# Half of a first stage's tiles transposed by DMA instead of TensorE, with q's relu on ScalarE and row statistics one tile per step

## The chip, the cores and the metric

The kernel runs on one core of one Trainium2 chip. The metric is the device time of one launch in microseconds (us). Before the change it was 854.06 us, the median of three runs (852.98 to 855.43). The span in a profile is some 2 us shorter than the time of the same execution.

## The reference, cut to what matters

One transformer block, forward and backward: linear attention of 32 heads and a gated MLP, each behind a layer norm without weights. Inputs are bf16; S is 2048, D is 640, F is 1728. The kernel returns the output and six gradients; the change touches only the beginning of the forward pass.

```python
def _A_ref(x, wqkv, wo):                      # x is already layer-normed
    qkv = (x @ wqkv) ...                      # split in q, k, v and heads
    phi = lambda t: jnp.where(t > 0, t + 1, jnp.exp(t)) + 1e-6
    pq, pk = phi(q), phi(k)
    kv = jnp.einsum("bhsd,bhse->bhde", pk, v)
    z = jnp.einsum("bhsd->bhd", pk)
    num = jnp.einsum("bhqd,bhde->bhqe", pq, kv)
    den = jnp.einsum("bhqd,bhd->bhq", pq, z)[..., None] + 1e-6
    o = num / den
    ...
h = x + _A_ref(_layernorm(x), A_wqkv, A_wo)
h2 = h + _B_ref(_layernorm(h), B_w1, B_w3, B_w2)   # silu(gate) * up, then w2
...
_out, _vjp = jax.vjp(_f, A_x, A_wqkv, A_wo, B_w1, B_w3, B_w2)
```

## The kernel before

Rows are handled in 16 tiles of 128. In the first stage each tile is normalised (`xn`, VectorE), transposed (`pqT`, TensorE and a ScalarE copy), and multiplied with wqkv. phi(k) and v stay in groups of four tiles for the kv products. phi(q) goes to DRAM (`pq_d`) and comes back transposed, in chunks of four tiles, by one DMA transposition each. `dma` and `dmaT` both issue from SyncE, so all these transfers stand in one queue in program order.

```python
    def p1_norm(t):
        xns[t] = p1.tile([P, D], BF16, name="xn", bufs=2)
        ln1.norm(xns[t][:], x_sb[:, t, :], t)

    def p1_tr(t):
        xn = xns.pop(t)
        tr = ps.tile([P, DT, P], BF16, name="tr", bufs=2)
        for c in range(DT):                               # DT = 5
            T.transpose(tr[:, c, :], xn[:, c * P:(c + 1) * P], ident[:])
        A.copy(out=pqT[:, :, t * P:(t + 1) * P], in_=tr[:])

    def phi(acc, dst):
        mq = p1.tile([P, D], BF16, name="mq", bufs=3)
        A.activation(two(mq[:]), acc[:, :, 0:HD], AF.Exp)
        V.tensor_scalar(out=mq[:], in0=mq[:], scalar1=1.0, scalar2=1e-6, op0=ALU.min, op1=ALU.add)
        V.scalar_tensor_tensor(out=two(dst), in0=acc[:, :, 0:HD], scalar=0.0, in1=two(mq[:]), op0=ALU.max,
                               op1=ALU.add)

    def q_store(t, pq):
        dma(out=pq_v[:, t, :], in_=pq)
        if t % TPC == TPC - 1:                            # TPC = 4
            load_pqT(t // TPC)                            # DMA transposition of 640 KB
    # ... cut: kv_group, zero_pads, the list of trickled weight loads ...
    for t in range(ST):                                   # ST = 16
        g, i = divmod(t, TPC)
        # ... cut ...
        k = p1_mm(t, D)
        if t + 2 < ST:
            p1_norm(t + 2)
        phi(k, pkc[g][:, i, :])
        if t + 1 < ST:
            p1_tr(t + 1)
        if i == 0 and g > 0:
            kv_group(g - 1, False)
        v = p1_mm(t, 2 * D)
        A.copy(out=va[g % 2]..., in_=v...)
        if 4 <= t < 12:
            q_tile(t - 4)
        if t % 2 == 0 and t + 4 < ST:
            ln1.run(x_sb, t + 4, t + 6)
        # ... cut ...
        if i == TPC - 1:
            dma(out=pk_v[:, sl, :], in_=pkc[g][:])
            dma(out=va_v[:, sl, :], in_=va[g % 2][:])
        elif t >= 2 and trickle:
            trickle.pop(0)()                              # the next weight load
```

After the MLP, the first weight gradient needs `hb`, a DMA transposition of 2 MB; the remaining products of the output run meanwhile on TensorE.

```python
    def load_hh(b):
        f0, fw = blk[b]
        hb[b] = U2.tile([P, ST, 512], BF16, name="hb", tag="ABCA"[b])
        dmaT(out=hb[b][:, :, 0:fw], in_=hh_d[f0:f0 + fw, :])

    load_hh(0)
    for _ in o2_steps(SC - 1, A.dma_start, "nd"):
        drain(1)
```

Of the kernel before, what the change touches and what calls it, by code (L numbers as in the profile page):

```python
# [9 lines left out]
P = 128  # L10
BF16 = mybir.dt.bfloat16
F32 = mybir.dt.float32
ALU = mybir.AluOpType
AF = mybir.ActivationFunctionType
# [4 lines left out]
S, D, H, F = 2048, 640, 32, 1728  # L19
# [3 lines left out]
ST, DT, CT = S // P, D // P, CP // P  # L23
FT, FP = 14, 1792
FL = F - 13 * P
W, SC, TPC = 512, 4, 4
HD = D // 2
# [36 lines left out]
def kernel(  # L64
# [19 lines left out]
    V, A, T, G, SY = nc.vector, nc.scalar, nc.tensor, nc.gpsimd, nc.sync  # L84
    dma, dmaT = SY.dma_start, SY.dma_start_transpose
# [22 lines left out]
    def pool(name, side="left", space=None):  # L108
        kw = dict(space=space) if space is not None else dict(side=side)
        return tc.alloc_tile_pool(name=name, bufs=1, reuse_waits="tile", **kw)  # L110
# [4 lines left out]
    x_sb = U1.tile([P, ST, D], BF16, name="x_sb", tag="S0")  # L115
# [32 lines left out]
    ln1, ln2 = Stats("ln1"), Stats("ln2")  # L148
# [3 lines left out]
    p1 = pool("p1", "right")  # L152
# [20 lines left out]
    def make_mask(m):  # L173
        a, b = M_H[m]
        v = mask[:, m, 0:M_W[m]]
        G.memset(v, 1.0)
        v = v.rearrange("p (h e) -> p h e", e=DA)

        G.affine_select(out=v, in_=v, pattern=[[-DH, b - a], [0, DA]], compare_op=ALU.is_ge, fill=0.0,
                        base=m * P - a * DH, channel_multiplier=1)  # L180
        G.affine_select(out=v, in_=v, pattern=[[DH, b - a], [0, DA]], compare_op=ALU.is_gt, fill=0.0,
                        base=a * DH + DH - m * P, channel_multiplier=-1)
# [6 lines left out]
    pqT = U1.tile([P, DT, S], BF16, name="pqT", tag="Q")  # L189
# [6 lines left out]
    def load_pqT(c):  # L196
        dmaT(out=pqT[:, :, c * W:(c + 1) * W], in_=pq_d[c * W:(c + 1) * W, :])
# [11 lines left out]
    pkc = {}  # L209
    xns = {}  # L210

    def p1_norm(t):
        xns[t] = p1.tile([P, D], BF16, name="xn", bufs=2)
        ln1.norm(xns[t][:], x_sb[:, t, :], t)

    def p1_tr(t):
        xn = xns.pop(t)
        tr = ps.tile([P, DT, P], BF16, name="tr", bufs=2)
        for c in range(DT):
            T.transpose(tr[:, c, :], xn[:, c * P:(c + 1) * P], ident[:])  # L220

        A.copy(out=pqT[:, :, t * P:(t + 1) * P], in_=tr[:])  # L222

    def p1_half(acc, t, n0):
        for c in range(DT):
            T.matmul(acc, lhsT=pqT[:, c, t * P:(t + 1) * P], rhs=wqkv[:, c, n0:n0 + HD], start=(c == 0),  # L226
                     stop=(c == DT - 1))

    def p1_mm(t, n0):
        acc = ps.tile([P, 2, 512], F32, name="big", bufs=3)  # L230
        for j in range(2):
            p1_half(acc[:, j, 0:HD], t, n0 + j * HD)
        return acc

    def two(ap):
        return ap.rearrange("p (j n) -> p j n", j=2)

    def phi(acc, dst):
        mq = p1.tile([P, D], BF16, name="mq", bufs=3)
        A.activation(two(mq[:]), acc[:, :, 0:HD], AF.Exp)  # L240
        V.tensor_scalar(out=mq[:], in0=mq[:], scalar1=1.0, scalar2=1e-6, op0=ALU.min, op1=ALU.add)
        V.scalar_tensor_tensor(out=two(dst), in0=acc[:, :, 0:HD], scalar=0.0, in1=two(mq[:]), op0=ALU.max,
                               op1=ALU.add)

    def q_store(t, pq):
        dma(out=pq_v[:, t, :], in_=pq)
        if t % TPC == TPC - 1:
            load_pqT(t // TPC)

    def q_tile(t):  # L250
        pq = p1.tile([P, D], BF16, name="pq", bufs=3)
        phi(p1_mm(t, 0), pq[:])
        q_store(t, pq[:])

    def kv_group(g, last):
        kv = ps.tile([P, 2, 512], F32, name="big", bufs=3)
        for i in range(TPC):
            for m, (a, b) in enumerate(M_H):
                bank, off = KV_SLOT[m]
                T.matmul(kv[:, bank, off:off + M_W[m]], lhsT=pkc[g][:, i, m * P:(m + 1) * P],  # L260
                         rhs=va[g % 2][:, i, a * DA:b * DA], start=(i == 0 and off == 0), stop=(i == TPC - 1),
                         skip_group_check=True)
        for bank, w in ((0, sum(M_W[0:3])), (1, sum(M_W[3:5]))):
            if g == 0:
                V.tensor_copy(out=kvacc[:, bank, 0:w], in_=kv[:, bank, 0:w])
            else:
                V.tensor_tensor(out=kvacc[:, bank, 0:w], in0=kvacc[:, bank, 0:w], in1=kv[:, bank, 0:w],
                                op=ALU.add)
        if last:
            for m, (a, b) in enumerate(M_H):  # L270
                bank, off = KV_SLOT[m]
                V.tensor_tensor(out=kvbd[:, m, a * DA:b * DA], in0=kvacc[:, bank, off:off + M_W[m]],
                                in1=mask[:, m, 0:M_W[m]], op=ALU.mult)
# [22 lines left out]
    for t in range(ST):  # L296
        g, i = divmod(t, TPC)
        if i == 0:
            pkc[g] = p1.tile([P, TPC, D], BF16, name="pkc", bufs=2)
        k = p1_mm(t, D)  # L300
        if t + 2 < ST:
            p1_norm(t + 2)
        phi(k, pkc[g][:, i, :])
        if t + 1 < ST:
            p1_tr(t + 1)
        if i == 0 and g > 0:
            kv_group(g - 1, False)
        v = p1_mm(t, 2 * D)
        A.copy(out=va[g % 2][:, i, 0:C].rearrange("p (j h e) -> p j h e", j=2, e=DA)[:, :, :, 0:DH],
               in_=v[:, :, 0:HD].rearrange("p j (h e) -> p j h e", e=DH))  # L310
        if 4 <= t < 12:
            q_tile(t - 4)
        if t % 2 == 0 and t + 4 < ST:
            ln1.run(x_sb, t + 4, t + 6)
        if 2 <= t < 2 + DT:
            make_mask(t - 2)
            G.memset(kvbd[:, t - 2, :], 0.0)
        if i == TPC - 1:
            sl = slice(g * TPC, (g + 1) * TPC)
# [3 lines that stand above are left out]
            trickle.pop(0)()  # L323
# [150 lines left out]
    def drain(n):  # L474
        for _ in range(min(n, len(later))):
            later.pop(0)()
# [74 lines left out]
    for c in range(SC):  # L551
        hhT[c] = pa.tile([P, FT, W], BF16, name="hhT", bufs=2)
        o2 = o2_steps(c - 1) if c > 0 else None

        def run_side(pos, fc):
            if c + 1 < SC:
                for f, i in sorted(sides[c][pos].get(fc, ()), key=lambda x: x[1]):
                    f((c + 1) * TPC + i)

        for fc in range(FT):  # L560
            mlp(c, fc, lambda: run_side(0, fc))
            drain(1)
            if o2 and not (c == SC - 1 and fc == 5):
                next(o2, None)
            run_side(1, fc)
            drain(1)
            if c == 0 and fc in (1, 4, 7):
                a, b = {1: (0, 4), 4: (4, 8), 7: (8, 13)}[fc]
                dma(out=w2[:, a:b, :], in_=B_w2[a * P:b * P, :].rearrange("(c p) n -> p c n", p=P))
                if fc == 7:  # L570
                    dma(out=w2[0:FL, FT - 1, :], in_=B_w2[(FT - 1) * P:F, :])
            if fc == (9 if c == 0 else 3) and c + 1 < SC:
                load_g2T(c + 1)
            if c == SC - 1 and fc == 0:
                g2 = U1.tile([P, ST, D], BF16, name="g2", tag="Q")
                tail = U2.tile([P, DT, P], BF16, name="w13tail", tag="g2T", bufs=2)
            if c == SC - 1 and fc in (1, 2, 5, 6):
                i = (1, 2, 5, 6).index(fc)
                dma(out=g2[:, i * TPC:(i + 1) * TPC, :], in_=goS[:, i * TPC:(i + 1) * TPC, :])
            if c == SC - 1 and fc == 8:  # L580
                dma(out=tail[:, :, 0:FL], in_=B_w1[:, F - FL:F].rearrange("(c p) f -> p c f", p=P))
                dma(out=tail[:, :, FL:P], in_=B_w3[:, 0:P - FL].rearrange("(c p) f -> p c f", p=P))
            if c == SC - 1 and fc == 9:
                woT = U1.tile([P, DT, D], BF16, name="woT", tag="W6")
                dmaT(out=woT[:], in_=A_wo[:, :])
# [71 lines left out]
    for fc in range(FT - 1):  # L657
# [3 lines left out]
        acc = ps.tile([P, 2, 512], F32, name="gw", bufs=4)  # L661
# [249 lines left out]
    a, b, c = ST - 1, ST - 2, ST - 3  # L911
# [34 lines left out]
    for m, (e0, e1) in enumerate(M_H):  # L946
        bank, off = KV_SLOT[m]
        V.tensor_tensor(out=gkv_b[:, m, e0 * DA:e1 * DA], in0=gkv[:, bank, off:off + M_W[m]],
                        in1=mask[:, m, 0:M_W[m]], op=ALU.mult)
# [65 lines left out]
    for t in range(ST):  # L1015
        c, i = divmod(t, TPC)
        acc = [d_acc(), d_acc()]
# [123 lines left out]
```

## Time and profile before

| What | Value | Where it is read |
|---|---|---|
| time | 854.06 us | median of three runs |
| span, TensorE busy | 851.9 us, 838.2 us | the page |
| TensorE idle at the start | 5.7 us | its list of waits |
| 20 to 72 us: TensorE, VectorE, ScalarE | 51.99, 38.04, 30.13 of 52 us | the table by stage |
| DMA share in the same stretch | 0.88 | the table by stage |

The lines themselves stand in the prediction below. They are read so: first who is busy all the time (TensorE), then in which stretch the change acts and what else is full there (the DMA), then what a transpose displaces on TensorE (0.28 us per tile). `nd` is the product that gives the reference's num and den.

### The profile page before, as it was taken

The numbers are of one execution on the slowest core, as the hardware profiler recorded it, in microseconds if no ns is written. First come the engines' busy times: TensorE is split into PE (matmuls) and PEld (weight loads), VectorE is DVE, ScalarE is ACT, GpSimd is POOL, SyncE is SP. The second block draws the span as 40 slices with busy tenths as digits, with TensorE's granted clock in tenths as the row PEclk, the third lists the DMA queues.
The fourth block names the chain that finished last, engine by engine and source line by source line (L and its number), as shares of the span: only waits on it lengthen the run. The fifth ranks groups of instructions, "written<-read, shape, count | busy, mean of one in ns | idle before, by whom it ended". The sixth has DMA issues, their size and how long they took to land.

```text
span 851.9 us, 14886 instructions
## 1 busy us (share of the span) xinstructions
PE 838.2 (98%) x5920; PEld 545.6 (64%) x5948; DVE 416.4 (49%) x945; ACT 322.2 (38%) x608; POOL 29.1 (3%) x51
## 2 busy tenths in 40 slices
PE   6999999999999999999999999999999999999998
PEld 4777654555555555777777777777877777655554
DVE  7786699778678566300146656654413343300000
ACT  4557866655555665011111111122522333311111
POOL 1410000000000000000000000000000000000000
PEclk9999999999999999999999999999999999999999
DMA  9979579364364465999789999979666897677671
GB/s 281 266 241 277 155 209 245 104 182 144 89 174 147 140 199 153 238 236 250 194 162 193 192 209 206 179 141 261 152 128 131 191 207 160 153 161 163 149 180 36
DMA packets 339573, 155.04 MB, mean 182 GB/s; under 512 B 242224, under 2 KB 338224, under 8 KB 339504
## 3 DMA queue, kind: packets, MB, share of 16 engines
q1 hardware_dynamic: 310688, 141.13, 68.4%
q10 hardware_dynamic: 28816, 12.97, 8.2%
q8 instruction: 46, 0.75, 0.4%
q14 instruction: 23, 0.19, 0.1%
HBM read 45.20 MB, written 50.02 MB: 112 GB/s over the span
## 4 chain that ended last, share of the span: by engine, by line
PE 85%; DMA 3%; DVE 2%; ACT 1%; issue 0%; SPq 0%; DVEq 0%; ACTq 0%
PE job L972 21%; PE mm L417 18%; PE ghn L720 11%; PE gxn L1062 8%; PE o L508 7%; PE gw L664 7%; PE gwo L827 3%; PE h L777 2%; PE at L374 2%; DMA ghT<-g_h 1%; DMA ggb<-gg_d 1%; PE mm L226 1%; PE dkv L1021 1%; DMA g2T<-in_grad_out_dram 1%; PE dkv L808 1%; PE h L808 1%
## 5 line engine op out<-in xcount | busy, mean ns | idle before, releaser
L972 PE MATMUL job<-gb,hnN 128*128 128x432 bf16 x640 | 117.0, 346 | 0.0
L720 PEld LDWEIGHTS <-ggb 128*128 128x128 bf16 x864 | 83.0, 98 | 31.6 <-DMA ggb<-gg_d 0.7
L972 PEld LDWEIGHTS <-hnN 128*128 128x128 bf16 x640 | 62.6, 98 | 54.1
L417 PE MATMUL mm<-pqT,w 128*128 128x512 bf16 x396 | 95.7, 379 | 0.5
L417 PEld LDWEIGHTS <-w 128*128 128x128 bf16 x540 | 52.4, 98 | 60.7 <-issue 0.2
L976 ACT CAST obs<-job 128x432 bf16<-128x432 f32 (+1 forms) x70 | 33.3, 475 | 123.8 <-PE job L972 123.8
L417 PE MATMUL mm<-g2T,w2T 128*128 128x512 bf16 x265 | 68.5, 379 | 1.4 <-DMA g2T<-in_grad_out_dram 0.7
L508 PE MATMUL o<-w,hhT 128*128 128x320 bf16 x448 | 67.5, 299 | 0.0
L1062 PE MATMUL gxn<-wqT,gT 128*128 128x320 bf16 x480 | 67.3, 299 | 0.0
L720 PE MATMUL ghn<-w13a,ggb 128*128 128x320 bf16 x448 | 65.6, 299 | 0.0
L720 PE MATMUL ghn<-w13b,ggb 128*128 128x320 bf16 x416 | 63.5, 299 | 0.4 <-DMA ggb<-gg_d 0.4
L226 PE MATMUL big<-wqkv,pqT 128*128 128x320 bf16 x400 | 58.6, 303 | 1.5 <-ACT pqT L222 0.8
L508 PEld LDWEIGHTS <-hhT 128*128 128x128 bf16 x448 | 43.8, 98 | 23.6
L226 PEld LDWEIGHTS <-pqT 128*128 128x128 bf16 x480 | 46.4, 99 | 19.5 <-issue 1.3
L1062 PEld LDWEIGHTS <-gT 128*128 128x128 bf16 x480 | 47.0, 98 | 18.2
L972 PEld LDWEIGHTS <-g 128*128 128x128 bf16 x480 | 46.6, 98 | 17.5
L664 PE MATMUL gw<-g,hb 128*128 128x320 bf16 x416 | 57.7, 299 | 0.0
L434 ACT CAST ghh<-mm 128x512 bf16<-128x512 f32 x56 | 32.8, 586 | 63.7 <-PE mm L417 62.3
L743 ACT ACTIVATE y<-wb,s,ln_rs 128x640 bf16<-128x640 f32 x32 | 29.5, 920 | 66.8 <-DVE wb L739 66.8
L664 PEld LDWEIGHTS <-hb 128*128 128x128 bf16 x416 | 40.3, 98 | 15.3
L731 ACT ACTIVATE gs<-ghn 128x640 bf16<-128x640 f32 x16 | 11.3, 704 | 88.4 <-PE ghn L720 75.3
L448 ACT ACTIVATE sig<-mm 128x512 bf16<-128x512 f32 x56 | 33.5, 598 | 28.9 <-PE mm L417 27.0
(138 smaller groups left out, 1067.1 us busy)
## 6 DMA issues: line engine op xcount, KB each, us to landing
hh_d<-hhT SPq DMA_DIRECT2D x24, 256.0 KB, 2.4
gg_d<-gate SPq DMA_DIRECT2D x24, 256.0 KB, 2.5
gg_d<-up SPq DMA_DIRECT2D x24, 256.0 KB, 2.2
ggb<-gg_d SPq DMA_DIRECT2D x6, 896.0 KB, 9.1
ggb<-gg_d SPq DMA_DIRECT2D x6, 832.0 KB, 7.8
out_dram<-obs ACTq DMA_DIRECT2D x40, 108.0 KB, 2.7
ggb<-gg_d SPq DMA_DIRECT2D x2, 1728.0 KB, 13.4
va_d<-va SPq DMA_DIRECT2D x4, 768.0 KB, 6.0
```

The lines of the kernel that those rows point to most:

```text
L226: T.matmul(acc, lhsT=pqT[:, c, t * P:(t + 1) * P], rhs=wqkv[:, c, n0:n0 + HD], start=(c == 0), stop=(c == DT - 1))
L417: T.matmul(acc[:], lhsT=w[:, c, fc * P:(fc + 1) * P], rhs=rhs[:, c, :], start=(c == 0), stop=(c == DT - 1))
L434: A.copy(out=ghh[n // 2][:, n % 2, :], in_=acc[:])
L448: A.activation(sig[:, i, :], gp[:], AF.Sigmoid)
L508: T.matmul(o2["ps"][:, 0:HD], lhsT=hhT[c][:, fc, i * P:(i + 1) * P], rhs=w2[:, fc, j * HD:(j + 1) * HD], start=(fc == 0), stop=(fc == FT - 1))
L664: T.matmul(acc[:, j, 0:HD], lhsT=hb[b][:, t, i * P:(i + 1) * P], rhs=g2[:, t, j * HD:(j + 1) * HD], start=(t == 0), stop=(t == ST - 1))
L720: T.matmul(acc[:, j, 0:HD], lhsT=ggb[t // 2][:, k, lo:lo + P], rhs=rhs[:, j * HD:(j + 1) * HD], start=(k == 0), stop=(k == NG - 1))
L743: A.activation(out=y[:], in_=wb[:], func=AF.Identity, bias=s[:, 3:4], scale=st.rs[:, t:t + 1])
L827: T.matmul(acc[m][:, j, 0:HD], lhsT=o_sb[:, t, m * P:(m + 1) * P], rhs=g_h[:, t, j * HD:(j + 1) * HD], start=(t == 0), stop=(t == ST - 1))
L972: T.matmul(acc[:, 0:n], lhsT=lhs[:, t, m * P:(m + 1) * P], rhs=rhs(t), start=(t == 0), stop=(t == ST - 1))
L976: A.copy(out=ob, in_=acc[:, 0:n])
L1062: T.matmul(acc[:, j, 0:HD], lhsT=gT[t][:, k, :], rhs=wqT[:, k, j * HD:(j + 1) * HD], start=(k == 0), stop=(k == 14))
```

## The change

The intent is to take 40 transposes off TensorE, which is busy 98% of the span, by letting DMA transpose the normalised tiles 8 to 15 straight into `pqT`. q's relu moves to ScalarE to unload VectorE. The statistics are spread one tile per step, and the loads of transposed q are moved out of the way of the new transfers. This is the whole diff, but for context lines.

```diff
+    XT_DMA = 8
+
     def p1_norm(t):
-        xns[t] = p1.tile([P, D], BF16, name="xn", bufs=2)
+        xns[t] = p1.tile([P, D], BF16, name="xn", bufs=4)
         ln1.norm(xns[t][:], x_sb[:, t, :], t)
+        if t >= XT_DMA:
+            dmaT(out=pqT[:, :, t * P:(t + 1) * P], in_=xns.pop(t)[:])
...
-    def phi(acc, dst):
+    def phi(acc, dst, relu=False):
         mq = p1.tile([P, D], BF16, name="mq", bufs=3)
         A.activation(two(mq[:]), acc[:, :, 0:HD], AF.Exp)
+        if relu:
+            rq = p1.tile([P, D], BF16, name="rq", bufs=3)
+            A.activation(two(rq[:]), acc[:, :, 0:HD], AF.Relu)
         V.tensor_scalar(out=mq[:], in0=mq[:], scalar1=1.0, scalar2=1e-6, op0=ALU.min, op1=ALU.add)
+        if relu:
+            V.tensor_tensor(out=dst, in0=mq[:], in1=rq[:], op=ALU.add)
+            return
...
     def q_store(t, pq):
         dma(out=pq_v[:, t, :], in_=pq)
-        if t % TPC == TPC - 1:
-            load_pqT(t // TPC)

     def q_tile(t):
         pq = p1.tile([P, D], BF16, name="pq", bufs=3)
-        phi(p1_mm(t, 0), pq[:])
+        phi(p1_mm(t, 0), pq[:], True)
...
-        if t + 2 < ST:
+        if t + 2 < XT_DMA:
             p1_norm(t + 2)
         phi(k, pkc[g][:, i, :])
-        if t + 1 < ST:
+        if t + 1 < XT_DMA:
             p1_tr(t + 1)
...
+        if XT_DMA <= t + 3 < ST:
+            p1_norm(t + 3)
+        if t + 4 < ST:
+            ln1.run(x_sb, t + 4, t + 5)
         if 4 <= t < 12:
             q_tile(t - 4)
-        if t % 2 == 0 and t + 4 < ST:
-            ln1.run(x_sb, t + 4, t + 6)
+        if t in (9, 13):
+            load_pqT((t - 9) // 4)
...
+            if c < 2 and fc == 11:              # in the MLP's loop
+                load_pqT(c + 2)
```

## The prediction

> **What bounds the kernel now.** I read first the page's busy shares and slices, then the table of busy time by stage, then TensorE's list of waits and its timeline in the first 98 us, which is the part the change touches, and last the DMA issuer's timeline there.
>
> Page of the kernel before, busy shares; then TensorE's waits in the first 98 us (us in total, times, longest):
>
> ```profile
> PE 838.2 (98%) x5920; PEld 545.6 (64%) x5948; DVE 416.4 (49%) x945; ACT 322.2 (38%) x608; POOL 29.1 (3%) x51
> ...
> PE tr L220 <- DVE xn L145: 5.7, 1, 5.7
> PE big L226 <- ACT pqT L222: 0.8, 1, 0.8
> PE big L226 <- DVE pkc L242: 0.4, 1, 0.4
> PE big L226 <- DMA wqkv<-in_A_wqkv_dram: 0.3, 1, 0.3
> ```
>
> TensorE is busy in 838.2 of 851.9 us. All its idle time is 13.7 us, and 5.7 of that is the start, before the first normalised tile exists. So a gain can only come from matmul work taken away; shorter chains elsewhere have next to no wait to shorten. In the table by stage (stretch, length, then busy time of each engine, clock, DMA share, GB/s) the first stage looks so:
>
> ```profile
> 0.00:20.00 20.00, 12.78 (x92) 8.79 (x93) 14.26 (x44) 7.92 (x11) 3.33 (x10) 1.00 0.99 280
> 20.00:72.00 52.00, 51.99 (x449) 39.24 (x448) 38.04 (x90) 30.13 (x45) 12.39 (x25) 1.00 0.88 252
> 72.00:98.00 26.00, 25.79 (x225) 18.80 (x227) 21.17 (x64) 20.49 (x50) 2.21 (x4) 1.00 0.73 228
> 98.00:150.00 52.00, 50.64 (x266) 24.96 (x271) 43.73 (x94) 36.74 (x68) 3.71 (x4) 1.00 0.82 211
> ```
>
> From 20 to 72 us TensorE never rests (51.99 of 52.00), VectorE is at 73%, ScalarE at 58%, DMA at 0.88. The DMA share is what the reader should keep: the transposes are to move onto the resource that is second fullest. What one transposition costs on TensorE is read from its timeline, by the distance of starts (start, length, what, count):
>
> ```profile
> 37.51 0.44 PE L220 MATMUL tr<-ident,xn 128*128 128x128 bf16 x5
> 37.79 4.24 PE L226 MATMUL big<-wqkv,pqT 128*128 128x320 bf16 x30
> 41.86 0.44 PE L220 MATMUL tr<-ident,xn 128*128 128x128 bf16 x5
> 42.14 1.49 PE L260 MATMUL big<-va,pkc 128*128 128x147 bf16 x20
> ```
>
> The five transposes of a tile start at 37.51 and the next matmul at 37.79: they displace 0.28 us. Their record lasts 0.44 us and the sum of their single durations is 5 x 219 ns = 1.1 us, but both of these count latency that overlaps.
>
> **What the Trainium skill says.** "TensorE: Matmul & The Clock Gate", section Wait - 56ns, not 53.3ns?, gives 55.6 ns from start to start at N = 128 on the warm array. The trace agrees: 0.28/5 = 56 ns. Its section Part 4: PE-mode transpose gives about 275 ns for a transpose in a kernel; here a record has 219 ns, and it is latency and not cost. "DMA: Bandwidth & Descriptors", section HWDGE ordering under Queues, rings and completion order: the issuer owns one ring on each engine, consumed in ring order. So a transposition issued behind a weight load waits for that load's bytes. The trace agrees: a 160 KB transposition of the o tiles lands 2.6 us (median) after its issue, but 6.1 us at the worst. "Advanced Engine Details and Errata", section X-Bar Transpose (TRN2), calls transposes as fast as ordinary DMAs; this trace does not fully agree: the 2.2 MB transposition of w2 took 18.1 us to landing, an estimated 122 GB/s in company with other loads, and four 640 KB ones of pq took 4.9 (median).
>
> **The change part by part.**
>
> Transposition of tiles 8 to 15. It removes 8 x 5 = 40 transposes from TensorE, 8 x 0.28 = 2.24 us, all from the stretch where TensorE is saturated, so all on the path. It also removes 8 PSUM copies on ScalarE (8 x 0.69 = 5.5 us), which are beside other work. It adds 8 DMA transpositions of 160 KB. The issuer is held about 1.23 us by each (the like transposition of hn takes 1.23), 9.8 us in all. Between 29 and 72 us that queue spends much time waiting for data, so it has room, but its order is strict.
>
> q's relu. Eight VectorE instructions of 825 ns (max with zero and add, read from PSUM) become bf16 adds as q of the later tiles already uses, 492 ns: 8 x 0.33 = 2.7 us off VectorE. ScalarE gets 8 relu passes; a like pass from PSUM (its exp of the same tile) takes 704 ns, so +5.6 us, against the 5.5 us of copies gone. In the steps for tiles 4 to 6 only the plus exists: exp, copy, copy of v, exp, relu are 5 x 0.7 = 3.5 us in a step of 4.35 us, which still fits. PSUM of q is freed about 0.5 us sooner. None of this is on the path.
>
> Statistics one tile per step. The same 475 ns passes, spread; some 6 more pairs of a small add (0.15 us, VectorE) and a power on the idle GpSimd (0.70 us). The one wait of TensorE on VectorE, 0.43 us at 17.2 us, comes just after VectorE did four statistics passes in a row in the first step; with two of them it should vanish: 0.4 us gained.
>
> Loads of pq transposed. Chunks 0 and 1 go two steps later; chunks 2 and 3 leave 85 and 101 us, where each holds the issuer 2.8 to 2.9 us, and go to the late part of the first two MLP chunks. Each is needed by the first nd product of the following chunk. In the trace these stand at 152.0 and 218.3 us; the stores just ahead of the new places were issued at 145.9 and 210.2. With 0.5 us of issue and the 4.9 us to landing, chunk 2 lands at about 151.4 (0.6 us to spare) and chunk 3 at 215.7 (2.6 to spare).
>
> The sum: 2.24 + 0.4 = 2.6 us at best, 0.3% of the time.
>
> **What may be given back: are the DMA transpositions in time?** The order of the issuer in the changed program, laid on this timeline (start, length of issue):
>
> ```profile
> 34.81 1.35 SPq L201 DMA_DIRECT2D w<-in_B_w_dram  x1
> 38.25 0.33 SPq L246 DMA_DIRECT2D pq_d<-pq  x1
> 38.64 0.43 SPq L204 DMA_DIRECT2D w<-in_B_w_dram  x1
> ...
> 66.82 0.57 SPq L320 DMA_DIRECT2D pk_d<-pkc  x1
> 67.49 0.46 SPq L321 DMA_DIRECT2D va_d<-va  x1
> ```
>
> Each tile is normalised three steps ahead, after k's phi, so some 8.5 us before its first use. Tile 9 follows the 864 KB load at 34.8 (5.7 us to landing): it lands near 42, needed near 44.5. Tile 11 follows the stores of pk and va (640 + 768 KB, 6.0 us to landing): about 51 to 52, needed about 53.5. Tile 13 comes behind the moved pq load (issue 2.8 us) and an 832 KB load: I get 61, needed 62. From there q is gone and steps shrink to about 3 us. Tile 15 stands behind the stores of pk and va of group 2, which go out near 62: I get 68, needed 67.4. So seven are in time by one to four us and the last by nothing. I charge an expected 0.8 us of waits of TensorE here, and 0.2 for pq chunk 2.
>
> **The rivals.** (1) Hidden or bare gain: all transpositions in time; then 854.06 - 2.6 = 851.5. For it: the margins above, and gaps in DMA around 46 and 60 to 66 us. (2) The DMA wait takes the place of the transposes: the DMA is at 0.88 and the eight add 1.3 MB to 13.1 MB in this stretch. If tiles 11, 13 and 15 each come 1 to 2 us late, the gain is gone: 854 to 856. For it: strict order behind large loads, worst landing 6.1 us; against it: the issuer's loads of w1 and w3 are only needed at 98 us and can slip. (3) ScalarE or VectorE becomes the bound in the first stage: 58% and 73% busy, both falling or level; I give it almost nothing. (4) The pq chunks moved late delay the MLP: the 2.8 us of issue hold up the stores of gate and up, whose buffers ScalarE wants two pairs on, and the first nd could wait: at most 1 us each. There is also the opposite, a freer queue at 85 to 104 us, but no TensorE wait of any size to collect there (1.36 us idle in 98 to 150, 0.7 of it the load of g2T).
>
> **Range and chances.** 854.06 - 2.6 + 0.8 + 0.2 is 852.5; I choose 852.3, since the large loads may well slip behind the small transposes. Runs of one kernel spread from 852.98 to 855.43, so over 1 us of the range is noise: 850.0 to 855.2. Two per cent is 17 us, over six times the whole cost of what is removed, and a loss of that size would need every transposition 2 us late: faster 0.01, same 0.97, slower 0.02.
>
> **What would show it right or wrong.** Right: 40 fewer transposes, the kv products of group 3 start about 2 us sooner than 72.33, TensorE's busy time near 836, and its waits on the DMA of the transposed tiles together under 1.5 us. Wrong by rival 2: a new line in TensorE's (or its weight loads') waits, on the DMA of pqT from xn, of 2 us or more. Wrong by rival 4: waits of nd on the load of pq near 150 us, or of ScalarE's gate on its store. The 0.4 us is shown by the vanished wait on pkc. The prediction fails above all if landings of the small transposes are far over 6 us.

## More of the kernel before

To follow the change through the whole program, four instructions serve as milestones in TensorE's timeline of the kernel before: the first kv product of group 3, the first MLP product, the first `nd` of the second chunk (`nd` is the product that gives the reference's num and den), and the first weight gradient (`gw`). The columns are start, length, engine, line, operation, what was written and read, sizes and count; a bracket at the end, where there is one, is the idle time just before and its releaser.

```profile
72.33 1.49 PE L260 MATMUL big<-va,pkc 128*128 128x147 bf16 x20
...
99.33 1.24 PE L417 MATMUL mm<-pqT,w 128*128 128x512 bf16 x5
...
152.00 0.52 PE L337 MATMUL nd<-kvbd,pqT 128*128 128x147 bf16 x6
...
354.95 4.51 PE L664 MATMUL gw<-g,hb 128*128 128x320 bf16 x32
```

None of the four has a bracket: TensorE did not wait at any of them.

## The result and the profile after

The changed kernel took 855.03 us (median of six runs, 854.15 to 856.69) against 854.68 us of the kernel before in the same rounds (six runs, 852.98 to 856.85). A ratio in this document is the mean time of one kernel's fast runs over the mean of the other's fast runs of the same rounds, so it is not quite the ratio of the medians quoted. Here it is 1.0007, with a 95% interval of 0.9989 to 1.0024. The time is inside the predicted range, but the gain of about 1.8 us that was forecast (854.06 to 852.3) did not come.

The page's busy line of the changed kernel, and then TensorE's longest waits (us in total, times, longest):

```profile
PE 837.7 (98%) x5908; PEld 543.3 (64%) x5908; DVE 415.5 (49%) x951; ACT 322.2 (38%) x608; POOL 31.7 (4%) x57
```

Against the kernel before the weight loads fell by 40, as they should, and the recorded matmuls only by 12 (5920 to 5908): some matmul records are missing, so the 0.5 us less of busy time says little about the gain. The waits:

```profile
PE tr L224 <- DVE xn L145: 5.6, 1, 5.6
PE big L230 <- DMA pqT<-xn: 1.4, 2, 1.1
PE gw L678 <- DMA hb<-hh_d: 1.1, 1, 1.1
PE big L230 <- ACT pqT L226: 0.8, 1, 0.8
...
PE nd L349 <- DMA pqT<-pq_d: 0.3, 1, 0.3
```

Three waits are new. 1.4 us are spent on the tiles that DMA transposes, 1.1 us on the load `hb` of the weight gradients at 355 us, which the change does not touch, and 0.3 us on the moved chunk of q. The waits of the kernel before on `pkc` (0.4) and on wqkv (0.3) are gone from this list, but they are gone from the list of its own repeat (r_before) as well. The table by stage, for the two stretches in which the change acts most (stretch, length, busy time of TensorE, weight loads, VectorE, ScalarE and GpSimd, clock, DMA share, GB/s):

```profile
20.00:72.00 52.00, 50.56 (x421) 37.65 (x419) 38.32 (x95) 30.20 (x45) 14.42 (x30) 1.00 1.13 287
72.00:98.00 26.00, 25.95 (x218) 18.18 (x216) 20.79 (x64) 21.07 (x52) 2.20 (x4) 1.00 0.57 189
```

TensorE, which never rested between 20 and 72 us, now rests 1.44 us there. The DMA share has gone from 0.88 to 1.13, so the packets' times together are longer than the stretch on all 16 DMA engines. TensorE's timeline of the changed kernel has the same four milestones, and before the first of them the two late tiles:

```profile
61.33 5.61 PE L230 MATMUL big<-wqkv,pqT 128*128 128x320 bf16 x40 [0.36 <-DMA pqT<-xn]
68.02 2.89 PE L230 MATMUL big<-wqkv,pqT 128*128 128x320 bf16 x20 [1.07 <-DMA pqT<-xn]
70.74 1.49 PE L268 MATMUL big<-va,pkc 128*128 128x147 bf16 x20
...
97.73 1.24 PE L429 MATMUL mm<-pqT,w 128*128 128x512 bf16 x5
...
150.84 0.53 PE L349 MATMUL nd<-kvbd,pqT 128*128 128x147 bf16 x6 [0.33 <-DMA pqT<-pq_d]
...
355.04 4.52 PE L678 MATMUL gw<-g,hb 128*128 128x320 bf16 x32 [1.07 <-DMA hb<-hh_d]
```

This execution is 1.59 us ahead at 72 us, 1.60 at the MLP, 1.16 at the second chunk, and then 0.09 behind at the first weight gradient. Part of the lead is luck of the start. The first kv product of group 0 began at 22.31 us here and at 23.18 before, and over all 18 traces it lies between 22.1 and 23.75. The two traces of the changed kernel alone have 22.31 and 23.63; most of that arises in 20 products of the first steps, which take 3.12 us in one (from 10.09 us) and 4.19 us in the other (from 10.34 us). So the experiments are judged by the distance from that product to the first MLP product. It is 76.15, 76.14, 76.15 and 76.13 us in the four traces whose first stage is the old one, and 75.42 here.

### The profile page after: what moved, and what is told of

It reads as the page before. It is cut to its first block, busy times and chain, and to the rows that moved or that the text cites. A ratio compares the mean times of both kernels' runs of the same rounds, so it can differ in the third digit from the quotient of the medians.

```text
span 852.4 us, 14861 instructions
## 1 busy us (share of the span) xinstructions
PE 837.7 (98%) x5908; PEld 543.3 (64%) x5908; DVE 415.5 (49%) x951; ACT 322.2 (38%) x608; POOL 31.7 (4%) x57
## 4 chain that ended last, share of the span: by engine, by line
PE 81%; DMA 6%; DVE 2%; ACT 1%; ACTq 0%; issue 0%; SPq 0%; DVEq 0%
PE job L986 21%; PE mm L429 18%; PE ghn L734 9%; PE gxn L1076 8%; PE gw L678 7%; PE o L520 6%; PE gwo L841 3%; PE at L386 2%; DMA ggb<-gg_d 2%; PE h L791 2%; DMA hb<-hh_d 2%; DMA ghT<-g_h 1%; PE mm L230 1%; PE dkv L1035 1%; PE dkv L822 1%; DMA pqT<-pq_d 1%
```

## The experiments

Sixteen runs were made, in four sets, each set on one chip with its own runs of the kernel before. The table has what their traces show, in us. "Stretch" is the distance just described; the waits are TensorE's. "Wait of nd on q" is for chunk 2, but for chunk 0 in e9 and e10.

| Kernel | stretch | wait on tiles | wait of nd on q | wait on hb | first gw at | ratio of times |
|---|---|---|---|---|---|---|
| before | 76.15 | - | 0 | 0 | 354.95 | |
| before, again (r_before) | 76.14 | - | 0 | 0 | 354.98 | 1.0005 |
| changed | 75.42 | 1.43 | 0.33 | 1.07 | 355.04 | 1.0007 |
| changed, again (r_after) | 76.32 | 2.35 | 0.83 | 0.54 | 357.02 | 0.9995 |
| e1_nodma | 73.79 | 0 | 0 | 1.24 | 354.64 | 0.9975 |
| e2_tr_only | 85.87 | 7.90 | 0 | 1.05 | 367.92 | 1.0119 |
| e3_relu_stats | 76.00 | - | 0 | 0 | 355.28 | 0.9996 |
| e4_pq_move | 76.14 | - | 0 | 0 | 354.86 | 0.9995 |
| e13_tr_pq | 79.15 | 2.20 | 1.13 | 1.35 | 360.21 | 1.0041 |
| e7_pad_after | 76.32 | 2.28 | 0 | 0 | 354.65 | 1.0002 |
| e8_pad_before | 76.15 | - | 0 | 0.80 | 357.17 | 1.0014 |
| e5_after_hb | 77.97 | 3.99 | 0 | 0 | 357.06 | 1.0015 |
| e9_order | 80.69 | 0 | 0.89 | 0.45 | 361.03 | 1.0087 |
| e10_all | 80.56 | 0 | 0.29 | 0 | 359.27 | 1.0043 |
| e11_order2 | 75.33 | 0 | 0 | 1.25 | 356.14 | 1.0005 |
| e12_all2 | 74.60 | 0 | 0 | 0 | 353.16 | 0.9976 |
| r_all2 | 74.79 | 0 | 0 | 0 | 352.79 | 0.9977 |
| e14_before_all | 76.13 | - | 0 | 0 | 354.01 | 0.9998 |

### What are 40 transposes worth? (e1_nodma)

The transpositions are replaced by copies of untransposed data on ScalarE. The result is wrong (relative error 0.85); only the time is of use.

```diff
         if t >= XT_DMA:
-            dmaT(out=pqT[:, :, t * P:(t + 1) * P], in_=xns.pop(t)[:])
+            A.copy(out=pqT[:, :, t * P:(t + 1) * P], in_=xns.pop(t)[:].rearrange("p (c q) -> p c q", q=P))
```

> The changed kernel with the 8 late tiles copied into place by ScalarE without any transposition (wrong result on purpose): TensorE loses the 40 transposes, the DMA gets nothing. Theory (the gain is real, 1.43 us of it is given back at late DMA transpositions, the rest stops at the join with the hb load at 355 us): the two waits on transposed tiles are gone, kv products of group 3 start near 69.3 us, TensorE comes to the first gw near 352.5, waits 2 to 3 us there for hb, and the time stays within 1 us of before. Rival (the hb wait of the changed kernel's profile is chance, hb lands when it is issued early enough): gw starts near 352.3 and the time is 2.5 us below before. Rival (DMA contention of the transpositions is the whole cost): also 2.5 us below.

Ratio 0.9975 (0.9957 to 0.9993). The two ends of the stretch, first in the kernel before and then in e1 (the second end of the former, 99.33, stands above):

```profile
23.18 1.49 PE L260 MATMUL big<-va,pkc 128*128 128x147 bf16 x20
```

```profile
23.61 1.49 PE L268 MATMUL big<-va,pkc 128*128 128x147 bf16 x20
...
97.40 1.24 PE L429 MATMUL mm<-pqT,w 128*128 128x512 bf16 x5
```

The stretch is 73.79 us, so 2.36 us are gained: the forecast 2.24 was right, and 2.36 is the bare gain used below. But its own trace reaches the first weight gradient only 0.31 us ahead of the kernel before, because it waits 1.24 us on `hb`, and it started 0.43 us later. So in that execution a join elsewhere took back half of what the first stage gained. In time, though, the theory missed: the six executions are 2.1 us below the kernel before by the ratio, near the 2.5 us of the rivals and not within 1 us.

### The parts alone (e2_tr_only, e3_relu_stats, e4_pq_move, e13_tr_pq)

e2 has the DMA transposition (T) without the moves of the q loads (P) and without relu and statistics (R). e3 has R alone, e4 P alone, e13 T and P.

```diff
 # e2, against the kernel before: p1_norm and the two bounds as in the change, nothing else
+        if t >= XT_DMA:
+            dmaT(out=pqT[:, :, t * P:(t + 1) * P], in_=xns.pop(t)[:])
 # e3, against the kernel before
-        phi(p1_mm(t, 0), pq[:])
+        phi(p1_mm(t, 0), pq[:], True)
-        if t % 2 == 0 and t + 4 < ST:
-            ln1.run(x_sb, t + 4, t + 6)
+        if t + 4 < ST:
+            ln1.run(x_sb, t + 4, t + 5)
 # e4, against the kernel before
-        if t % TPC == TPC - 1:
-            load_pqT(t // TPC)
+        if t in (9, 13):
+            load_pqT((t - 9) // 4)
+            if c < 2 and fc == 11:
+                load_pqT(c + 2)
 # e13, against the changed kernel
-        phi(p1_mm(t, 0), pq[:], True)
+        phi(p1_mm(t, 0), pq[:])
-        if t + 4 < ST:
-            ln1.run(x_sb, t + 4, t + 5)
+        if t % 2 == 0 and t + 4 < ST:
+            ln1.run(x_sb, t + 4, t + 6)
```

> Before plus the DMA transposition of tiles 8 to 15 alone (pq loads where they were, relu on VectorE, statistics in pairs). Theory: as in the changed kernel, 40 transposes fewer; waits on transposed tiles of 1 to 4 us, more than the 1.43 us of the changed kernel because pq chunk 0 now stands in the queue before tile 12 or 11; time 0 to 2 us over before. Rival (the moved pq loads and not the transpositions cost): waits below 1 us and time 1 to 2 us below before.

> Before plus q's relu on ScalarE and one-tile statistics alone. Theory: the 0.43 us wait on pkc at 17.2 us goes, all later milestones to 335 us move 0.4 to 0.8 us forward, and the hb join takes it: time within 1 us of before. Rival (ScalarE's extra passes cost): new waits on PSUM in the first stage, time over before by 1 us or more.

> Before plus the later places of the four pq loads alone. Theory: stage 1 as before, one new wait of nd on pq chunk 2 near 152 us of 0.2 to 0.5 us, nothing else; time within 1 us of before. Rival (freeing the issuer at 85 to 104 us is worth something, or the late place costs stores and ScalarE): a shift of over 1 us either way by 218 us.

> The changed kernel without q's relu on ScalarE and without one-tile statistics: transpositions and moved pq loads alone. Theory (both other parts are off the path): waits on transposed tiles within 1 us of the changed kernel's 1.43 us, time within 1.5 us of it. Rival (the relief of VectorE is what lets the transposed tiles come in time): new waits on VectorE's pq and pkc, over 1 us, later normalised tiles, and 2 us or more over the changed kernel.

| Parts | ratio of times |
|---|---|
| R (e3) | 0.9996 (0.9974 to 1.0019) |
| P (e4) | 0.9995 (0.9974 to 1.0015) |
| T (e2) | 1.0119 (1.0100 to 1.0139) |
| T + P (e13) | 1.0041 (1.0027 to 1.0055) |
| T + P + R (changed) | 1.0007 and 0.9995 |

Alone, R and P are worth nothing, as forecast for R, and the wait of `nd` that was expected of e4 did not come. Beside the DMA transposition P is worth 0.8% (T against T + P), and R is worth 0.4% beside both. e2's waits on tiles, 7.90 us, are far above the 1 to 4 us expected of it. So "none of this is on the path" holds only in the kernel that the statement was read from. In e2 the reason is visible at the issuer (start, length of issue):

```profile
67.78 2.68 SPq L197 DMA_TRANSPOSE pqT<-pq_d  x1
70.52 0.57 SPq L326 DMA_DIRECT2D pk_d<-pkc  x1
71.19 0.45 SPq L327 DMA_DIRECT2D va_d<-va  x1
71.74 2.81 SPq L218 DMA_TRANSPOSE pqT<-xn  x1
```

The last small transposition is issued only at 71.74 us, behind the 640 KB load of q and two stores, and TensorE's timeline shows what that costs:

```profile
78.39 4.32 PE L230 MATMUL big<-wqkv,pqT 128*128 128x320 bf16 x20 [5.75 <-DMA pqT<-xn]
```

In e13 the loads are out of the way. Its waits on the tiles (2.20 us) are no worse than those of the changed kernel, but TensorE also waits on VectorE's phi: 0.31 us on `pkc` and 0.19 and 0.95 us on `pq`. The last of these, in its timeline:

```profile
44.89 16.84 PE L230 MATMUL big<-wqkv,pqT 128*128 128x320 bf16 x120 [0.95 <-DVE pq L252]
```

The stretch of e13 is 2.8 us longer than that of the changed kernel run again. The labelled waits on VectorE explain 1.45 us of it; the rest carries no label. So it was the rival named for e13 that came. T with R but without P was not run.

### The small transpositions in the strict queue (r_after, e9_order, e11_order2)

The changed kernel was run again, and its issuer's order was altered twice. The issuer's timeline of the changed kernel, ahead of the two late tiles, is what the orders start from:

```profile
51.16 3.63 SPq L197 DMA_TRANSPOSE pqT<-pq_d  x1
54.84 0.57 SPq L204 DMA_DIRECT2D w<-in_B_w_dram  x1
55.51 1.21 SPq L218 DMA_TRANSPOSE pqT<-xn  x1
...
60.06 0.44 SPq L332 DMA_DIRECT2D pk_d<-pkc  x1
60.60 0.51 SPq L333 DMA_DIRECT2D va_d<-va  x1
61.60 1.77 SPq L218 DMA_TRANSPOSE pqT<-xn  x1
```

Tile 13's transposition (55.51) stands behind the q chunk and a load of w3. Tile 15's (61.60) stands behind the stores of `pk` and `va`. Those are just the two tiles that TensorE waited for. e9 and e11 both put the stores of group 2 after the last small transposition, and they move the q chunks in different ways.

```diff
 # e9, against the changed kernel
-        if t in (9, 13):
-            load_pqT((t - 9) // 4)
+        if t == 12:
+            store_kv(2)          # pk and va of group 2, one step later
+        if t == 13:
+            load_pqT(0)
+    load_pqT(1)                  # after the last weight load
 # e11, against the changed kernel
+        if t == 11:              # in q_store, right after q tile 11 is stored
+            load_pqT(1)
-        if t in (9, 13):
-            load_pqT((t - 9) // 4)
+        if t == 12:
+            load_pqT(0)
+            store_kv(2)
 # both: the third chunk's load one step sooner
-            if c < 2 and fc == 11:
+            if c < 2 and fc == (10, 11)[c]:
```

> The changed kernel again, for a second trace and more rounds. Theory: waits on transposed tiles of 1.2 to 2.5 us in total, instruction fetch near 350 us, hb lands 12.8 to 13.2 us after its issue and a wait of about 1 us at the first gw; from the first kv product to the first MLP product about 75.4 us. Rival (the hb wait of the first trace was chance): hb lands in 11.2 to 11.6 us and no wait. Time equal to before within 1.5 us either way.

> The changed kernel with three reorderings of its DMA queue: pq chunks 0 and 1 and the stores of pk and va of group 2 go behind the last transposition, pq chunk 2 one step sooner. Theory: the waits on transposed tiles (0.36 and 1.07 us) and on pq chunk 2 (0.33) are gone, from the first kv product to the first MLP product it takes 73.8 us as with no DMA transposition at all, 75.4 in the changed kernel; the hb wait stays at 1.0 to 1.3 us; time 1.5 to 2 us below the changed kernel. Rival (DMA bandwidth and not the order): waits of over 1 us stay or move to wo or to nd of the first tiles.

> The changed kernel with pq chunk 0 and the pk and va stores of group 2 behind the last transposition, chunk 1 beside the late q tiles (where the kernel before had chunk 2), chunk 2 one MLP step sooner. Theory: no wait on transposed tiles and none at the late q tiles; first kv to first MLP product in 73.8 to 74.2 us (75.4 in the changed kernel); hb wait of 0.8 to 1.3 us remains; time about 1.5 us below the changed kernel. Rival (any place for the pq loads costs as much as it frees): 75 us or more for that stretch.

The repeat of the changed kernel gave 0.9995 (0.9977 to 1.0012) and waits on tiles of 2.35 us. Together with e7 and e5 below, which leave this order alone, there are four traces of it: 1.43, 2.35, 2.28 and 3.99 us, on average 2.5. That is the whole bare gain of 2.36.

Both new orders removed these waits: from the first kv product of group 0 to that of group 3 took 46.65 us in e9 and 46.63 in e11, against 46.80 in e1, where these tiles are not transposed by DMA. Yet e9 was slower, 1.0087 (1.0066 to 1.0108). The issuer's timeline of e9 shows where my order was bad:

```profile
66.08 6.52 SPq L197 DMA_TRANSPOSE pqT<-pq_d  x1
...
75.00 8.21 SPq L197 DMA_TRANSPOSE pqT<-pq_d  x1
83.31 1.01 SPq L256 DMA_DIRECT2D pq_d<-pq  x2
```

The 640 KB transposition held the issuer for 8.21 us. The stores of late q tiles stood behind it, so VectorE waited 6.5 us for a `pq` buffer, and TensorE 4.6 us for `hn`. e11 put that load where its data has just become ready. It lost less, but its stretch is still 1.5 us above e1's, with 1.5 us of a wait on `hn`; 75.33 us is what its rival had said (75 or more), not its theory. Its time, 1.0005 (0.9985 to 1.0026), also has a wait of 1.25 us on `hb`.

### The join at 355 us (e7_pad_after, e8_pad_before, r_before)

In the changed kernel the chain of waits passes through a transfer for which the kernel before did not wait:

```profile
335.77 6.18 PE o L520 x46
341.94 13.05 DMA hb<-hh_d
355.04 4.52 PE gw L678 x32
```

The load was issued 1.15 us sooner than before (341.94 against 343.09), as TensorE's lead would have it, but it landed after 13.0 us instead of 11.2. The landing times are from the view of DMA issues, first of the kernel before, then of the changed kernel:

```profile
hb<-hh_d SPq DMA_TRANSPOSE x1, 11.2
```

```profile
hb<-hh_d SPq DMA_TRANSPOSE x1, 13.0
```

With 11.2 us the load had landed at 354.3, only 0.5 us before its first weight load at 354.82. A lead of TensorE alone does not use this slack up: in both kernels the load is issued 6.34 us after the last 134 products of the output begin (336.75 before, 335.60 after), so its issue and its need move together. DMA throughput from 341 to 357 us, in 40 slices of 0.4 us (GB/s), of the kernel before:

```profile
GB/s 266 10 120 197 279 302 69 138 51 129 148 10 156 289 291 290 289 291 290 289 292 357 209 288 284 292 289 289 292 339 344 313 387 377 135 45 141 157 282 291
```

And the same of the changed kernel:

```profile
GB/s 195 220 302 59 126 21 171 254 291 289 269 251 282 289 291 291 289 324 246 245 243 211 150 285 317 95 3 9 69 298 160 318 386 383 329 184 102 259 290 289
```

The changed kernel has a hole in the tail of the transfer, from about 351.0 to 352.6 us (95, 3, 9, 69 GB/s). In the kernel before the low slices lie at the head of the transfer, up to 345.8 us. Up to 1.4 us before each hole there is one packet group of the instruction queue. The entry of that queue, of the kernel before between 344.00 and 344.25 us, and of the changed kernel between 350.50 and 350.75 us (fetches, MB, share):

```profile
q8 instruction: 1, 0.02, 30.0%
```

```profile
q8 instruction: 1, 0.02, 25.9%
```

That is a fetch of TensorE's instructions, 46 in the whole program with 0.75 MB by the page, so 16 KB each. (TensorE has 11,868 recorded instructions there, one fetch for about 258, which is why the queue is taken to be TensorE's.) The Trainium skill, "Runtime: NRT & Kernel Launch", section Instruction fetch mechanics, says that instructions come in blocks of 16 KiB, 256 at a time, through a DMA queue of the engine's own. The sizes in the trace agree. The change removed 40 transposes, which are 40 weight loads and 40 matmuls, 80 instructions. So every later block boundary falls 80 instructions later in the program. Here TensorE runs 134 recorded matmuls in 18.36 us, with a weight load each, so 80 instructions are an estimated 5.5 us; the trace has the fetch 6.5 us later by the clock, and 7.7 us later counted from the load's issue (8.7 us after it instead of 1.0). The count gives the direction and the rough size; the 2 us that it lacks are not explained. This is a claim that can be tested: put 80 instructions back where TensorE idles anyway, and the wait on `hb` must go; put 176 into the kernel before, which is 80 short of a block, and the wait must come.

```diff
     zero_pads()
+    pad = ps.tile([P, DT, P], BF16, name="tr", bufs=2)
+    for n in range(40):          # e7, in the changed kernel; 88 in e8, in the kernel before
+        T.transpose(pad[:, n % DT, :], ident[:], ident[:])
     ln1.run(x_sb, 0, 1)
```

> The changed kernel with 40 transposes of the identity that nobody reads, put on TensorE in its idle time before the first tile: its instruction stream has again as many instructions ahead of the hb join as before (80 more). Theory (the hb load lands 13 instead of 11.3 us after its issue in the kernels with 80 TensorE instructions fewer, because a 16 KB instruction fetch of TensorE then falls into its last part): the fetch is at 343 to 345 us again, hb lands about 11.3 us after its issue, no wait at the first gw. Rival (the hb wait comes from TensorE arriving earlier, or from the moved DMAs): a wait of 1 us or more stays. The time is 1 to 2 us below the changed kernel; some of that is the array already warm at the start, so the landing decides and not the time.

> The kernel before with 88 such transposes at the start: 176 instructions more, which moves the 256-instruction fetches to where the changed kernel has them. Theory: a fetch at about 350 us of the old count falls into hb's last part, hb lands near 13 us after its issue, a wait of 1.0 to 1.5 us at the first gw that the kernel before has not. Rival: no wait, hb lands after 11.3 us.

> The kernel before again, for a second trace. Theory: instruction fetch near 344 us, hb lands 11.2 to 11.6 us after its issue, no wait at the first gw; from the first kv to the first MLP product 76.15 us. Rival (hb wait is chance): a wait of 0.5 us or more. Ratio to before 1.000 within its interval, which shows the noise of these comparisons.

Both came. e7's `hb` landed after 11.6 us without a wait, with the fetch about 1 us after the load's issue. e8's landed after 12.8 us, and TensorE waited, in a kernel whose first stage and DMA queue are those of the kernel before:

```profile
357.17 4.52 PE L667 MATMUL gw<-g,hb 128*128 128x320 bf16 x32 [0.80 <-DMA hb<-hh_d]
```

The throughput of e8 from 341 to 357 us has the same hole, now at 353.4 to 354.6 us:

```profile
GB/s 0 20 18 300 10 161 182 233 305 56 128 21 118 188 205 292 287 285 292 289 289 292 289 343 230 287 182 291 289 319 131 1 10 42 295 97 288 385 390 373
```

Over all traces with the load at its old place, a fetch 1.0 to 1.1 us after its issue goes with a landing of 11.2 to 11.6 us and no wait (before, its repeat, e3, e4, e7). A fetch in its tail, 8.2 to 9.2 us after the issue, goes with 12.4 to 13.3 us and a wait of 0.45 to 1.35 us (the changed kernel, its repeat, e1, e2, e8, e9, e11, e13). e7 also shows that a lead passes the join when the landing is short: its load is issued 0.30 us sooner than in the kernel before, and its first weight gradient starts 0.30 us sooner, without a wait. Why a fetch should stop the transposition is not shown, nor why it costs more in the tail: the head of the transfer is slow in every trace, and not all of that is the fetch's work (e1 has a slice of 6 GB/s there with no fetch near). In time, e7 gave 1.0002 (0.9983 to 1.0020), e8 1.0014 (0.9994 to 1.0033), and the kernel before against itself 1.0005 (0.9987 to 1.0022). The wait is shown by traces, then; a loss of 0.1% is too small for the intervals, and the 1 to 2 us that were expected of e7 in time did not come.

### Letting the gain through (e10_all, e5_after_hb, e12_all2, e14_before_all, r_all2)

The cure for the join is a load of `hb` that starts two MLP steps sooner, into a buffer that is free by then. e5 is the changed kernel with this alone. e10 is e9 with it and with the 40 extra transposes of e7, e12 is e11 with both, and r_all2 is e12 again, in another set. e14 has both in the kernel before, without any part of the change.

```diff
-        hb[b] = U2.tile([P, ST, 512], BF16, name="hb", tag="ABCA"[b])
+        hb[b] = U2.tile([P, ST, 512], BF16, name="hb", tag="CABC"[b])
...
+            if c == SC - 1 and fc == 12:     # in the MLP's loop; load_hh is defined ahead of it
+                load_hh(0)
...
-    load_hh(0)
```

> The reordered kernel with the first hb load issued two MLP steps sooner (into the buffer that is free first) and the 40 warming transposes at the start. Theory: no wait on transposed tiles, none at hb; the gains add: 2.4 us (transposes) plus 0.4 to 1.2 (start), so 2.5 to 4 us below before. Rival (a later DMA bound takes any gain back): time within 1 us of before, with the waits on gT, ghT or gg loads grown by what was gained.

> The changed kernel with the first hb load two MLP steps sooner and nothing else. Theory: no hb wait, TensorE reaches the first gw at 353 to 355.5 us as its own work allows; time 0.5 to 1.2 us below the changed kernel. Rival (the load only moves the queue's congestion): a new wait of the same size on the stores' buffers or on the second hb load.

> The same order with the earlier hb load and 40 warming transposes at the start. Theory: the gains add up at the end: first gw near 351, no hb wait, time 2.5 to 4 us below before. Rival (a later load takes it back): first gw near 351 but the first of the last weight gradient jobs still starts at 731 to 732 us.

> The kernel before with the earlier hb load and the 40 warming transposes, and none of the change. Theory (the combined version's gain comes from the change, now let through): at most 1 us below before, from the warm start. Rival (the warm start is the whole gain of the combined version): as fast as the combined version, about 2 us below before.

> The combined version again: order of the pq loads and stores, earlier hb load, warm start. Theory: again 1 to 3.5 us below before, first gw near 353, no hb wait. Rival (its first result was luck): ratio to before of 0.999 or more.

In none of the five is there a wait on `hb`. e5, without the new order, gained nothing: 1.0015 (0.9994 to 1.0037). Its list of TensorE's waits names the reason, 4.0 us on the tiles:

```profile
PE tr L224 <- DVE xn L145: 5.7, 1, 5.7
PE big L230 <- DMA pqT<-xn: 4.0, 2, 2.6
```

Its first `gw`, at 357.06 us, is later than the 353 to 355.5 expected. So removing the second cause without the first does not help, as removing the first without the second (e11, 1.0005) does not. e10 kept e9's fault and gave 1.0043 (1.0024 to 1.0062). e12, with both causes removed, gave 852.22 us against 855.09, 0.9976 (0.9957 to 0.9994). Its repeat gave 853.16 against 854.21, 0.9977 (0.9962 to 0.9992). The first weight gradient in the timeline of r_all2, without a bracket:

```profile
352.79 4.51 PE L689 MATMUL gw<-g,hb 128*128 128x320 bf16 x32
```

That is 2.16 us sooner than in the kernel before. e14 gave 0.9998 (0.9982 to 1.0014): the early load and the extra transposes do nothing measurable for the time of a kernel that does not have the change, and r_all2's mean time is 1.8 us below e14's in the same set. So the gain needs the change. But not all of the 2.16 us is the transposes': r_all2's first kv product already starts 1.07 us sooner than that of the kernel before (22.11 against 23.18), and e14's, with the same extra transposes, 0.41 sooner (22.77). Against e14 the lead at the first weight gradient is 0.85 us in e12 and 1.22 us in r_all2, and the stretch is shorter by 1.53 and 1.34 us. Neither e12 without the extra transposes nor its order of the queue without the DMA transposition was run, so that the gain is the bare gain of the 40 transposes let through is argued and not shown. Against the kernel before, the combined version gains 0.2%, which is small, but both intervals lie below 1; e12 expected 2.5 to 4 us and got 2.1 by its ratio. Its mean is 1.7 us below that of the changed kernel in the same set, a difference whose interval just reaches 0.

### What stays open

From 415 to 560 us TensorE waits on `ghT` and `ggb`, and those waits vary by about 3.5 us from trace to trace with no tie to the change; in e4, for one, the two on `ghT` came to 1.93 and 1.56 us, and its span is 855.4 us although it was level with the kernel before at 355 us. With one trace per run, the milestones up to 355 us are firmer than any span. e1's time gained 2.1 us by its ratio, while its trace shows only 0.31 us at the first weight gradient; whether its other executions were spared the wait on `hb` is not known.

## Why the prediction went wrong

It was wrong. The mechanism of the gain was right, and the size of the give-back was not.

- **The bare gain: right.** Forecast were 2.24 us for the transposes; e1 shows 2.36.
- **The 0.4 us at 17.2 us: the wait vanished, but no gain in time can be shown.** The wait on `pkc` is absent from the changed kernel's list and from e3's. That alone proves little, since the repeat of the kernel before has none either: TensorE came to this place only at 16.91 us there, and at 17.50 us in e3. But of the two kernels with the early load and the extra transposes, e14, which has no part of the change, waits there, and r_all2, which has it, does not, though it comes sooner:

```profile
16.78 2.88 PE L226 MATMUL big<-wqkv,pqT 128*128 128x320 bf16 x20 [0.44 <-DVE pkc L242]
```

```profile
16.12 2.88 PE L230 MATMUL big<-wqkv,pqT 128*128 128x320 bf16 x20
```

  Still, e3's first kv product starts at 23.50 us against 23.18 before. The start varies by 1.6 us over the traces, four times the amount.
- **"I charge an expected 0.8 us of waits of TensorE here": this step failed.** The tiles named were the right ones, 13 and 15. The first came after its need where a margin of 1 us had been worked out, the second later than by the 0.6 us worked out. In four traces the waits were 1.43, 2.35, 2.28 and 3.99 us, 2.5 on average. By the prediction's own sign (under 1.5 us together) the first trace alone would have passed; the other three show its rival 2. The error is in the landing times. Counted from the first kv product of group 0, so that the start drops out, tile 13 was to land after 37.8 us (61 less 23.18) and tile 15 after 44.8; in the four traces they landed after 38.5 to 41.3 and after 45.7 to 48.2 us. Even the issue of the eight took 11.2 us in the first trace instead of 9.8. The medians of transfers with less in front of them were laid on a queue that holds more. The small transpositions landed after 5.4 us in the median and 6.4 at worst in the changed kernel's first trace, and after 8.1 at worst in e5. The 2.8 us of issue for the q chunk were 3.63 and, in e5, 5.88. That is rival 2, which was given with 854 to 856 us, and it is what happened.
- **"0.2 for pq chunk 2": about right.** The wait was 0.33 and 0.83 us in the two traces of the changed kernel and none in e7 and e5, which leave this order alone: 0.3 us on average. Elsewhere with the load at this place it was 1.13 in e13 and none in e1 and e4. There is none in e11 and e12, which issue the load one step sooner.
- **Relu and statistics, "None of this is on the path": true alone, false in combination.** e3 gives 0.9996. But T and P without R cost 0.41%, about 3.5 us, and with R they cost nothing. VectorE's 73% were an average of the kernel before, and no slack to be left out of the sum. That it is the tiles' normalisation a step sooner which uses VectorE's slack up is argued, not tested.
- **What the prediction did not have: the join at 355 us.** The landing of `hb` had some 0.5 us of slack, and with the shifted fetch it came 1.3 to 1.8 us later, so 1.07 and 0.54 us were waited. A lead of TensorE alone would have passed, since the load's issue moves with it (e7). e7 and e8 show the cause in both directions.

The sum with measured terms (bare gain, tiles, chunk 2, `hb`) is −2.36 + 1.43 + 0.33 + 1.07, or 0.5 us on the slow side, in the first trace of the changed kernel, and −2.36 + 2.35 + 0.83 + 0.54, or 1.4 us, in the second. The two timings gave +0.6 and −0.4 us by their ratios, each with an interval of about 1.5 us either way. The terms come from single traces and do not simply add, since time lost early moves the later joins as well. The chance of 0.97 for "within 2%" was right.

## What to carry to other kernels

Work taken off a saturated engine can be given back at every later transfer that lands just in time, so list those of small slack, the ones that show no wait at all included, and ask of each two things: does its issue move with the engine (then a lead alone passes), and can its landing grow longer? A small transfer on a strict queue is to be charged with the landing times of what stands ahead of it in the new order, at their worst rather than their median, and a large DMA transposition belongs where its data is ready and nothing urgent follows. Adding or removing instructions moves all later instruction fetches of that engine; where one falls into a transposition on the path, a few idle instructions elsewhere are a cheap test of it.

## What the Trainium skill lacked or had wrong

- "Runtime: NRT & Kernel Launch", Instruction fetch mechanics, calls the cost of crossing a block of 256 instructions mostly hidden. That is said of the engine; for a transfer it is not so here: a fetch in the tail of a 2 MB DMA transposition left the DMA at 3 and 9 GB/s for two slices of 0.4 us, and the landing took 12.4 to 13.3 us instead of 11.2 to 11.6. No page says that fetches and transpositions disturb each other.
- "Advanced Engine Details and Errata", X-Bar Transpose (TRN2), gives no time for which the issuing queue is held, and elsewhere in the skill there are only counts of sequencer cycles for "previous generations". A 160 KB transposition held it for at least 1.2 us (a 160 KB store for at least 0.33 us), and one of 640 KB for 2.5 us at best and 8.21 us in e9.
- The same section calls transposes as fast as ordinary transfers. These runs do not show it wrong: in the kernel before, the 160 KB transpositions of the o tiles landed after 2.6 us and the 160 KB stores of the same tiles after 2.1 us (medians), and the 18.1 us that the prediction holds against it were measured in the company of other loads. What the section does not say is how little that helps in a full queue: those of the change landed after 5.4 us in the median and up to 8.1 us behind loads and stores of some 640 to 860 KB; for a dependent engine the queue ahead of it, more than its own speed, is what counts.
